# Attention's scores, masks and values' products in 64x64 quarters of the TensorE array

## The chip, the core and the metric

The kernel runs on one core of one Trainium2 chip. The metric is the device time of one execution in microseconds (us); less is better. Three runs of the kernel before gave 774.86, 775.87 and 775.99 us, median 775.87 us.

Names of engines in the profile: PE is TensorE (matmuls), PEld its weight loads, DVE is VectorE, ACT is ScalarE, POOL is GpSimd, SP is SyncE, which here only issues DMAs.

## What is computed

Routed attention feeds a mixture of experts. Cut to what matters:

```python
# B=4, H=8, S=768, D=64, 16 clusters; q, k, v in float32
q_assign = argmax(q_n @ c_n.T); k_assign = argmax(k_n @ c_n.T)   # nearest centroid, per head
scores = (q @ k.T) / 8
scores = where(q_assign[:, None] == k_assign[None, :], scores, -1e9)
attn = softmax(scores)
x = (attn @ v)  ->  rows of (B*S, H*D) = (3072, 512)
expert_idx = argmax(unit(x) @ unit(expert_emb).T / tau)          # 8 experts
out[rows of e] = gate * (relu(x @ w1[e]) @ w2[e])                # w1: 512x1024, w2: 1024x512
```

## The kernel before

**Tiling of the attention.** Two heads of one batch make a *pair*: 16 pairs (`NP`). A pair has two halves of the 768 queries (384 each, `HS`), and each half has six blocks of 128 keys (`NJ`). One half of the queries of one pair with one key block is a *unit*: 192 units, in groups of six (one half of the queries). Scores stand with the keys on the partitions: for each of the two heads a 128 x 384 matrix.

A unit has three steps:

- `scores(i)` (L434 to L454) writes the PSUM tile `s_ps` (128 x 2 x 512, pool `psS`, two buffers). For each head `h` one bfloat16 matmul adds the mask (`kH` and `hot`, numbers of the clusters written so that unequal clusters give a hugely negative sum) and one float32 matmul adds `k q` (L448). Each contracts over 64 rows (the head's 64 partitions) and gives 128 columns of the array; the two heads lie on the two halves of the array's rows.
- `expo(i)` (L456 to L459): one ScalarE exponential of 128 x 768 from `s_ps` to `prob` in SBUF (pool `pp`, five buffers).
- `attend(i)` (L461 to L492): for each head a float32 matmul with the 128 keys on the rows and 64 columns adds `v prob` to the PSUM tile `o_ps` (L468; pool `psO`, two buffers of one 512-column bank). Both heads share one bank; head `h` has partitions 64h to 64h+63. VectorE sums the probabilities over the key blocks into `acc` (L477 for the first two blocks, L487 for each further one). After the sixth block ScalarE copies `o_ps` (128 x 384) to `o_sb` (L492).

`total` (L494) sums `acc` over the keys by matmuls with ones (L508) and takes reciprocals; GpSimd spreads them (L531). `divide` (L535) adds the mean of `v` times a tiny number, multiplies by the reciprocals (L546) and writes `xT`. `rows` (L557) turns `xT` and writes the rows of x to HBM (`x_rows`).

**Order of the work.** The order on every engine is written out by hand in the loop from L1089 on: one iteration takes two units. It emits `scores` and `expo` of the next two units, then `between` (L1020), then `attend` of its own two units. So PE alternates between two units of scores and two of values' products, two units ahead with the scores. Six iterations (`it` 0 to 5) make a pair `n`. `between` puts the other work into the gaps: at `it` 0 the products that choose the clusters of pair n+1 (L330), at `it` 1 `choose` (VectorE, then ScalarE writes `cd`, and SP issues the DMA that transposes it to `hot`, L361), at `it` 3 `rows` and `keys` (GpSimd copies `hot` to `kH`, L386), at `it` 4 and 5 the transposes of q and k of pair n+2 (VectorE, L324) and `values` (three GpSimd adds, L395 to L397). `divide` of the pair before comes at `it` 2, ahead of the `attend` of that iteration. The router's work on a finished batch (`route_pieces`, L575: products L587, logits L600, reading rows back, norms, gates) is spread over the next batch's iterations by the number m = 6*nb + it, and the places of the first tokens (`early`, L996) over the last two batches. Each engine runs its list in order and waits at semaphores.

**The experts.** After the attention, blocks of 128 tokens go through the two layers: `hidden` (L944, matmuls L954) and `result` (L963, matmuls L970). The output tile `y_ps` comes from the same pool `psO` as `o_ps`.

Of the kernel before, what the change touches and what calls it, by code (L numbers as in the profile page):

```python
# [9 lines left out]
F32 = mybir.dt.float32  # L10
# [8 lines left out]
P = 128  # L19
# [20 lines left out]
def kernel(  # L40
# [88 lines left out]
    xip = ctx.enter_context(tc.tile_pool(name="xip", bufs=3))  # L129
    psO = ctx.enter_context(tc.tile_pool(name="psO", bufs=2, space=PSUM))  # L130
    psM = ctx.enter_context(tc.tile_pool(name="psM", bufs=2, space=PSUM))
    at = ctx.enter_context(ExitStack())
    ldp = at.enter_context(tc.tile_pool(name="ldp", bufs=2, side="right"))
# [44 lines left out]
    en_r = smp.tile([E, 1], F32, name="en_r", bufs=1)  # L178
    idle_ps = psO.tile([P, 4, P], F32, tag="o_ps", name="idle_ps")

    def keep_up(n):

        for _ in range(n):
            nc.tensor.matmul(
                idle_ps, lhsT=onesb, rhs=bc(onesb, [P, 4, P], 1), start=True, stop=True
            )
# [247 lines left out]
    def scores(i, parts=(0, 1)):  # L434

        n, hq, j = units[i]
        t = ld[n]
        if "s_ps" not in un[i]:
            un[i]["s_ps"] = psS.tile([P, 2, 512], F32, tag="s_ps", name="s_ps")
        s_ps = un[i]["s_ps"]  # L440
        for part in parts:
            if part == 0:
                l, r = t["kH"], t["H"][:, :, SQ * hq : SQ * hq + SQ]
            else:
                l, r = t["kT"], t["qT"][:, HS * hq : HS * hq + HS]
            for h in range(2):
                rows = slice(D * h, D * h + D)
                nc.tensor.matmul(  # L448
                    s_ps[:, h, 0:HS],
                    lhsT=l[rows, P * j : P * j + P],  # L450
                    rhs=r[rows],
                    start=part == (1 if len(parts) < 2 else 0),
                    stop=part == (0 if len(parts) < 2 else 1),
                )  # L454

# [5 lines left out]
    def attend(i):  # L461

        n, hq, j = units[i]
        d, g = un[i], gr[i // GU]
        if j == 0:
            g["o_ps"] = psO.tile([P, 512], F32, tag="o_ps", name="o_ps")
        for h in range(2):
            nc.tensor.matmul(  # L468
                g["o_ps"][D * h : D * h + D, 0:HS],
                lhsT=ld[n]["v"][:, j, h],  # L470
                rhs=d["prob"][:, h],
                start=(j == 0),
                stop=(j == NJ - 1),
            )
        if j == 1:
            g["acc"] = xp.tile([P, 2, HS], F32, tag="acc", name="acc", bufs=3)
            nc.vector.scalar_tensor_tensor(  # L477
                out=g["acc"],
                in0=un[i - 1]["prob"],
                scalar=NJ * EPS,  # L480
                in1=d["prob"],
                op0=ALU.add,
                op1=ALU.add,
            )
            un[i - 1].clear()
        elif j > 1:
            nc.vector.tensor_tensor(g["acc"], g["acc"], d["prob"], ALU.add)  # L487
            d.clear()
        if j == NJ - 1 and n + 1 < NP:
            if hq == 0:  # L490
                ld[n]["o_sb"] = xp.tile([P, 2, HS], F32, tag="o_sb", name="o_sb", bufs=1)
            nc.scalar.copy(ld[n]["o_sb"][:, hq], g["o_ps"][:, 0:HS])  # L492

# [41 lines left out]
    def divide(*gs):  # L535
# [5 lines left out]
        if G == 2:  # L541
# [5 lines left out]
            out=xT[pairs[n]][:, hq : hq + G],  # L547
            in0=ld[n]["o_sb"] if G == 2 else d["o_ps"][:, 0:HS].unsqueeze(1),
            scalar=ld[n]["ev"],
# [413 lines left out]
    def result(j, halves=(0, 1)):  # L963
        d = mo[j]
        for half in halves:
            if half == 0:
                d["y_ps"] = psO.tile([P, DM], F32, tag="o_ps", name="y_ps")
            bk = d["y_ps"]
# [51 lines left out]
    def between(n, it):  # L1020
# [27 lines left out]
        if b > 0:  # L1048
# [4 lines left out]
            m = NJ * nb + it  # L1053
            if m in (5, 9, 12):
                read((m - 5) // 3 * 2, (m - 5) // 3 * 2 + 2)
            if m in (8, 9, 11, 12, 14, 15):
                norms((8, 9, 11, 12, 14, 15).index(m))
            if (nb, it) == (0, 3):
                products(0)
            elif (nb, it) == (0, 4):  # L1060
                products(1)
            elif (nb, it) == (1, 2):
                logits(0)
            elif (nb, it) == (1, 3):
                logits(1)
            elif (nb, it) == (1, 4):
                choose()
            if 16 <= m < 20:
                gates[m - 16]()
        if n == NP - 1 and it == 4:  # L1070
# [16 lines left out]
    with tc.manual_schedule(engines=by_hand):  # L1087
        begin()
        for i in range(0, len(units), 2):  # L1089
# [16 lines left out]
            between(n, it)  # L1106
            if it == 2 and n > 0:
                divide(2 * n - 2, 2 * n - 1)
            elif it == 4 and n == NP - 1:
                divide(2 * n)  # L1110
# [8 lines left out]
            for m in range(i, i + 2):  # L1119
                attend(m)  # L1120
            if i + 2 == len(units):
                rows(ngroups - 2)
                route[b][0](0)
# [15 lines left out]
        total(ngroups - 1)  # L1139
        divide(ngroups - 1)  # L1140
        rows(ngroups - 1)
        hidden(0, (1,))
# [118 lines left out]
```

## Time and profile before

| what | number |
|---|---|
| median of three runs | 775.87 us |
| time of the profiled execution | 775.89 us |
| span of its instructions | 774.0 us |
| granted TensorE clock | 0.997 of full |
| PE matmuls | 752.9 us busy (97%), 4782 |
| DVE | 333.5 us busy (43%), 546 |
| ACT | 270.0 us busy (35%), 444 |
| POOL | 281.9 us busy (36%), 394 |

The attention takes the first 363.7 us of the span: the first matmul of the experts (L954) starts there. The span runs from the program's first instruction to its last. A row of the groups reads: line, engine, operation, output<-inputs, shape, number of instructions | busy us of all, mean ns of one | idle us of the engine before them and who ended it. Shapes such as `64*128 64x384` of a matmul are the rows and columns of the array in use, and the partitions and columns of the moving data. One float32 matmul of the program is two matmul records in the trace (768 records on L468 for 192 units of two matmuls). A busy time of PE is a union of overlapping records: a matmul record of 482 ns starts its successor after a shorter step, so lengths of steps are read from the starts.

### The profile page before, as it was taken

To read this page: it belongs to the slowest core of one execution; us is meant where nothing else is said; L and a number is where in the kernel's file an instruction comes from. 1 tells how busy PE (TensorE), PEld (TensorE's weight loads), DVE (VectorE), ACT (ScalarE), POOL (GpSimd) and SP (SyncE) were. 2 spreads that over 40 slices of the span, in tenths; PEclk is the share of its full clock that TensorE was granted. 3 is DMA by queue.
4 is the path that set the end of the run, shared out by engine and by line. 5 is a ranking of instruction groups with operands and counts; after the bars stand their busy time and mean duration, and the time that the engine had idled before them with its cause. 6 is when DMAs were issued, how large, how long until landed. Compare 5 with 4: busy or idle time off the path is not lost. (4 is left out here: it accounts for less than half of the span.)

```text
span 774.0 us, 12547 instructions
## 1 busy us (share of the span) xinstructions
PE 752.9 (97%) x4782; PEld 438.5 (57%) x4782; DVE 333.5 (43%) x546; ACT 270.0 (35%) x444; POOL 281.9 (36%) x394
## 2 busy tenths in 40 slices
PE   7999999999999999999999999999999999999995
PEld 3444444444344334445777668677677786776862
DVE  5688887888788898888440100000000000000000
ACT  5555555675556645673151111111111111111110
POOL 3233322532343223455054335445344353453211
PEclk9999999999999999999999999999999999999998
DMA  9457768987989586559799967799877665146300
GB/s 154 75 126 143 149 98 127 194 154 96 151 158 190 81 103 110 116 132 212 198 346 267 385 243 259 259 335 340 279 257 250 223 222 204 42 150 245 123 15 24
DMA packets 247582, 140.00 MB, mean 181 GB/s; under 512 B 209621, under 2 KB 209621, under 8 KB 247520
## 3 DMA queue, kind: packets, MB, share of 16 engines
q1 hardware_dynamic: 237712, 117.08, 61.6%
q0 software_dynamic: 6432, 13.66, 5.0%
q10 hardware_dynamic: 3376, 8.44, 4.1%
q8 instruction: 39, 0.64, 0.4%
q14 instruction: 23, 0.19, 0.1%
HBM read 158.40 MB, written 13.64 MB: 222 GB/s over the span
## 5 line engine op out<-in xcount | busy, mean ns | idle before, releaser
L954 PEld LDWEIGHTS h_ps<-xTm,w1s 128*128 128x128 f32 x1792 | 204.3, 192 | 15.4 <-issue 12.7
L954 PE MATMUL h_ps<-xTm,w1s 128*128 128x128 f32 x1792 | 205.5, 275 | 1.6 <-DVE xTm L942 1.6
L970 PE MATMUL y_ps<-w2s,hT 128*128 128x512 f32 x448 | 197.0, 593 | 0.0
L459 ACT ACTIVATE prob<-s_ps 128x768 f32<-128x768 f32 x192 | 152.3, 811 | 106.1 <-PE s_ps L448 92.7
L448 PE MATMUL s_ps<-qT,kT 64*128 64x384 f32 x768 | 155.1, 482 | 0.0
L468 PE MATMUL o_ps<-prob,v 128*64 128x384 f32 x768 | 145.1, 499 | 0.0
L970 PEld LDWEIGHTS y_ps<-w2s,hT 128*128 128x128 f32 x448 | 83.0, 190 | 93.7 <-issue 93.7
L932 DVE STREAM_TRANSPOSE xTm<-xin 128x512 f32<-128x512 f32 x22 | 15.6, 711 | 272.9 <-remote 190.0
L487 DVE TENSOR_TENSOR acc<-acc,prob 128x768 f32<-128x768 f32 x128 | 129.5, 1012 | 6.8 <-ACT prob L459 0.5
L961 ACT ACTIVATE hT<-h_ps 128x512 f32<-128x512 f32 x56 | 33.4, 597 | 210.3 <-PE h_ps L954 121.8
L870 POOL DMA_INDIRECT xin<-x_rows,pidx x88 | 88.8, 1009 | 30.3 <-issue 28.1
L468 PEld LDWEIGHTS o_ps<-prob,v 128*64 128x64 f32 x768 | 46.6, 136 | 83.6 <-issue 79.7
L981 POOL DMA_INDIRECT out_dram<-y,sidx x24 | 24.4, 1017 | 169.2 <-ACT y L980 163.3
L531 POOL COPY inv<-inv 32x12 f32<-32x12 f32 x120 | 40.9, 341 | 123.4 <-DVE inv L528 117.3
L448 PEld LDWEIGHTS s_ps<-qT,kT 64*128 64x128 f32 x768 | 68.7, 189 | 20.6 <-issue 20.2
L448 PE MATMUL s_ps<-hot,kH 64*128 64x384 bf16 x384 | 63.5, 328 | 6.6 <-ACT prob L459 4.1
L980 ACT ACTIVATE y<-y_ps,gatein 128x512 f32<-128x512 f32 x28 | 19.2, 687 | 128.8 <-PE y_ps L970 122.0
L448 PEld LDWEIGHTS <-kH 64*128 64x128 bf16 x384 | 19.5, 93 | 73.1 <-issue 53.3
L386 POOL COPY kH<-hot 128x768 bf16<-128x768 bf16 x15 | 16.1, 1074 | 84.6 <-DMA hot<-cd 80.9
L870 POOL DMA_INDIRECT gatein<-gate_rows,gidx x28 | 29.3, 1045 | 8.4 <-issue 8.4
L477 DVE SCALAR_TENSOR_TENSOR acc<-prob 128x768 f32<-128x768 f32 x32 | 30.1, 940 | 0.0
L395 POOL TENSOR_TENSOR vs<-v 128x384 f32<-128x384 f32 x16 | 23.0, 1440 | 2.6 <-DMA v<-in_v_dram 2.6
(205 smaller groups left out, 416.2 us busy)
## 6 DMA issues: line engine op xcount, KB each, us to landing
w1s<-in_moe_w_dram SPq DMA_DIRECT2D x28, 2048.0 KB
w2s<-in_moe_w_dram SPq DMA_DIRECT2D x28, 2048.0 KB
v<-in_v_dram SPq DMA_DIRECT2D x32, 192.0 KB
q<-in_q_dram SPq DMA_DIRECT2D x60, 96.0 KB
k<-in_k_dram SPq DMA_DIRECT2D x60, 96.0 KB
x_rows<-xb SPq DMA_DIRECT2D x60, 96.0 KB
xr<-x_rows SPq DMA_DIRECT2D x9, 512.0 KB
w1s<-in_moe_w_dram ACTq DMA_DIRECT2D x4, 1024.0 KB
```

Of the source, the lines that this page charges most:

```text
L395: nc.gpsimd.tensor_tensor(vs, v[:, 0 : NJ // 2], v[:, NJ // 2 :], ALU.add)
L448: nc.tensor.matmul(s_ps[:, h, 0:HS], lhsT=l[rows, P * j : P * j + P], rhs=r[rows], start=part == (1 if len(parts) < 2 else 0), stop=part = ...
L459: nc.scalar.activation(d["prob"], d["s_ps"][:, :, 0:HS], ACTF.Exp, scale=scale)
L468: nc.tensor.matmul(g["o_ps"][D * h : D * h + D, 0:HS], lhsT=ld[n]["v"][:, j, h], rhs=d["prob"][:, h], start=(j == 0), stop=(j == NJ - 1),)
L477: nc.vector.scalar_tensor_tensor(out=g["acc"], in0=un[i - 1]["prob"], scalar=NJ * EPS, in1=d["prob"], op0=ALU.add, op1=ALU.add,)
L487: nc.vector.tensor_tensor(g["acc"], g["acc"], d["prob"], ALU.add)
L531: nc.gpsimd.tensor_copy(inv2[M * to : M * to + M, :, i % 2], inv[M * i : M * i + M])
L870: nc.gpsimd.indirect_dma_start(out=to, out_offset=None, in_=of, in_offset=bass.IndirectOffsetOnAxis(ap=at, axis=0), bounds_check=n - 1, oo ...
L954: nc.tensor.matmul(bk[:, m : m + P], lhsT=w1s[j % 2][:, c, f0 + m : f0 + m + P], rhs=d["xT"][:, P * c : P * c + P], start=(c == 0), stop=( ...
L961: nc.scalar.activation(d["hT"][:, f0 : f0 + 512], bk, ACTF.Relu)
L970: nc.tensor.matmul(bk, lhsT=d["hT"][:, P * c : P * c + P], rhs=w2s[j % 2][:, c], start=(c == 0), stop=(c == KF - 1),)
L981: nc.gpsimd.indirect_dma_start(out=out[:], out_offset=bass.IndirectOffsetOnAxis(ap=to, axis=0), in_=y, in_offset=None, bounds_check=N - 1, ...
```

## The change

All three kinds of attention matmuls are cut into quarters of 64 rows by 64 columns of the array.

- **Scores and masks**: the 128 keys of a unit are taken as two halves of 64; each half goes to its own partitions of `s_ps`. Two matmuls (one for each head) become four.
- **Values' products**: each half of the keys is contracted on its own, half 0 into the first bank of `o_ps`, half 1 into the second. Two matmuls become four, and the two partial sums are added later.
- **PSUM**: `o_ps` is now two banks, in one buffer instead of two buffers of one bank. `y_ps` of the experts gets a pool of its own (`psY`, two buffers), opened in the same place when `psO` is closed after the last `divide`.
- **The sum of the halves**: after a group's last block ScalarE copies both banks (128 x 768 instead of 128 x 384) to `o_sb`, and a new function `unite` adds the halves into `o_sum`: on GpSimd for 15 pairs, on VectorE for the last. `divide` reads `o_sum`. For the last pair there was no copy before (`divide` read PSUM); now there is.
- **Order**: `divide` of the pair before comes after the `attend` of `it` 2 instead of ahead of it; the router's products come one iteration later, and its reading, norms and gates three.

```diff
-            for h in range(2):
-                rows = slice(D * h, D * h + D)
-                nc.tensor.matmul(
-                    s_ps[:, h, 0:HS],
-                    lhsT=l[rows, P * j : P * j + P],
...
+            for half in range(2):
+                for h in range(2):
+                    rows = slice(D * h, D * h + D)
+                    nc.tensor.matmul(
+                        s_ps[D * half : D * half + D, h, 0:HS],
+                        lhsT=l[rows, P * j + D * half : P * j + D * half + D],
...
-            g["o_ps"] = psO.tile([P, 512], F32, tag="o_ps", name="o_ps")
+            g["o_ps"] = psO.tile([P, 2, 512], F32, tag="o_ps", name="o_ps")
...
+            for half in range(2):
+                keys = slice(D * half, D * half + D)
+                nc.tensor.matmul(
+                    g["o_ps"][D * h : D * h + D, half, 0:HS],
+                    lhsT=ld[n]["v"][keys, j, h],
+                    rhs=d["prob"][keys, h],
...
-        if j == NJ - 1 and n + 1 < NP:
-            if hq == 0:
-                ld[n]["o_sb"] = xp.tile([P, 2, HS], F32, tag="o_sb", name="o_sb", bufs=1)
-            nc.scalar.copy(ld[n]["o_sb"][:, hq], g["o_ps"][:, 0:HS])
+        if j == NJ - 1:
+            t = ld[n]
+            t["o_sb"] = xp.tile([P, 2, HS], F32, tag="o_sb", name="o_sb", bufs=1)
+            nc.scalar.copy(t["o_sb"], g["o_ps"][:, :, 0:HS])
+
+    def unite(g):
+        n, hq, _ = units[GU * g]
+        t = ld[n]
+        if hq == 0:
+            t["o_sum"] = xp.tile([P, 2, HS], F32, tag="o_sum", name="o_sum", bufs=1)
+        add = (nc.gpsimd if n + 1 < NP else nc.vector).tensor_tensor
+        add(t["o_sum"][:, hq], t["o_sb"][:, 0], t["o_sb"][:, 1], ALU.add)
...
-            if it == 2 and n > 0:
-                divide(2 * n - 2, 2 * n - 1)
-            elif it == 4 and n == NP - 1:
+            if it == 4 and n == NP - 1:
                 divide(2 * n)
...
             for m in range(i, i + 2):
                 attend(m)
+            if it == 2:
+                if n > 0:
+                    divide(2 * n - 2, 2 * n - 1)
+                unite(2 * n)
+            elif it == 5:
+                unite(2 * n + 1)
...
-    psO = ctx.enter_context(tc.tile_pool(name="psO", bufs=2, space=PSUM))
+    psO = ato.enter_context(tc.tile_pool(name="psO", bufs=1, space=PSUM))
```

## The prediction

> **What bounds the kernel now.** I read the busy times first, then the stretches pair by pair, then PE's waits, then PE's order of time in a pair without other work. In the page's first part only PE is full:
>
> ```profile
> PE 752.9 (97%) x4782; PEld 438.5 (57%) x4782; DVE 333.5 (43%) x546; ACT 270.0 (35%) x444; POOL 281.9 (36%) x394
> ```
>
> An average hides stages, so next the stretches, cut at the first mask matmul of each pair (columns: stretch, its length, busy us and records of PE, PEld, DVE, ACT, POOL, granted clock, DMA share, GB/s). A quiet pair, the three in which PE pauses, and one more with much on VectorE:
>
> ```profile
> 75.80:96.70 20.90, 20.90 (x148) 8.76 (x146) 17.49 (x24) 11.32 (x17) 6.85 (x12) 1.00 0.75 144
> ...
> 182.80:206.80 24.00, 22.55 (x166) 9.11 (x166) 19.25 (x26) 12.20 (x19) 4.13 (x10) 1.00 0.88 138
> ...
> 249.70:272.70 23.00, 21.27 (x150) 8.94 (x150) 20.62 (x42) 14.05 (x21) 6.21 (x12) 1.00 0.54 83
> 272.70:297.00 24.30, 22.60 (x164) 9.06 (x162) 22.30 (x37) 12.75 (x20) 7.90 (x13) 1.00 0.76 97
> ...
> 318.80:340.10 21.30, 21.30 (x161) 9.12 (x160) 18.79 (x31) 14.22 (x26) 8.25 (x17) 1.00 0.46 107
> ```
>
> PE never pauses in the quiet pair, and VectorE is 84% busy. PE pauses for 1.45, 1.73 and 1.70 us in three pairs. The waits of PE over the whole span say for whom:
>
> ```profile
> PE s_ps L448 <- ACT prob L459: 4.1, 4, 1.7
> ...
> PE s_ps L448 <- POOL kH L386: 1.4, 1, 1.4
> ```
>
> The first is ScalarE being late, because VectorE is late with `acc` and so holds the `prob` buffers (two pairs from 249.7 us), or because it loads tables there; the second is the mask's DMA landing late. So the attention is bound by PE's own steps in 13 pairs. How much of these is streaming? Two iterations of a quiet pair in PE's order of time (start, us, operation):
>
> ```profile
> 64.91 1.51 PE L468 MATMUL o_ps<-prob,v 128*64 128x384 f32 x8
> 66.35 0.34 PE L448 MATMUL s_ps<-hot,kH 64*128 64x384 bf16 x2
> 66.53 0.81 PE L448 MATMUL s_ps<-qT,kT 64*128 64x384 f32 x4
> 67.17 0.33 PE L448 MATMUL s_ps<-hot,kH 64*128 64x384 bf16 x2
> 67.33 0.81 PE L448 MATMUL s_ps<-qT,kT 64*128 64x384 f32 x4
> 68.07 1.51 PE L468 MATMUL o_ps<-prob,v 128*64 128x384 f32 x8
> ```
>
> Read starts, not lengths. Four score records take 66.53 to 67.17 = 0.64 us: two rounds of two concurrent heads, 0.32 each. A mask round is 67.33 - 67.17 = 0.16. `attend` of two units is eight records, four rounds, so 1.28 us of streaming, yet the next kind begins after 1.44: 0.16 lost. The second unit's scores should take 0.64, and `attend` begins after 0.74: 0.10 lost. The first mask step is 0.18, 0.02 over. Within one shape almost nothing is lost, though bfloat16 follows float32 and one head's weights the other's. The loss is where 64x128 gives way to 128x64 and back: about 0.10 us each way, and a further 0.05 inside `attend` (its second round comes late, the first weight load after the change having had nothing to hide under).
>
> **The change, part by part.**
>
> *Quarters.* Each round now has four records instead of two, the same streaming: four halves of work on four quarters, if they run at once. Nothing before uses row and column halves together. For it: two row halves at once (L448), two column halves at once (L468), and four column quarters at once: L330 streams eight float32 records of 384 columns, two rounds of four, 0.64 us, and takes 0.78 with the change of shape. So I take 0.32 per float32 round and 0.16 per mask round as before, 2.88 us for an iteration that now takes 68.07 - 64.91 = 3.16. By the code's list, values' products are followed directly by masks in some 79 of 96 iterations (not where `total` comes between), and scores directly by values' products in some 65 (not around the cluster products, router or experts' steps). The sum is 79 x 0.10 + 65 x (0.095 + 0.052) = 7.9 + 9.6 = **17.5 us**. Bounds of the unknown: the gain cannot pass 96 x 0.28 = 27 us; below, if two quarters of the same rows run one after the other, each unit takes 1.44 us more, 192 x 1.44 = 276 us lost. I take the near rows, which show concurrency in both directions.
>
> *Weight loads*: 20 matmul records per unit instead of 10, each with a load. Loads of one shape overlap streaming today (four `attend` rounds with loads of 133 to 137 ns take no longer than their streaming, but for the first), so 0. The densest issue in the trace is L508: 16 records within 0.81 us, about 50 ns each; the masks would need 40. A bound from above: 10 ns short on four masks, 192 x 0.04 = 8 us.
>
> [...]
>
> *ScalarE's copy and one buffer of `o_ps`.* The next group's first `attend` must wait for the copy. In the trace a copy that waits for PE alone starts 0.11 us after the next mask does (277.84 against 277.73). It takes 0.48 us now, and 0.81 at 128 x 768 (the exponential of that size). The next `attend` comes 1.62 us after that mask. It ends at 0.92, 0.7 us early: cost 0. Behind it on ScalarE stand two exponentials, whose scores end later still. If ScalarE is one exponential behind (0.81), PE waits 0.1, 31 times, 3 us; two behind, 28 us. ScalarE is 54% busy in the quiet pair. The copy sheds its wait for `divide`, 14.6 us of ScalarE's today.
>
> *`unite`* adds two GpSimd adds per pair of L395's size, 1.0 to 1.7 us. GpSimd has room (7 of 21 us), and the result is wanted three iterations later. Ahead of `keys` and `values` it delays them by its own length at most: `keys` waits for its DMA today (81 us in all), so 0. But it slows VectorE:
>
> ```profile
> L487 DVE TENSOR_TENSOR acc<-acc,prob x128: 908/957/1649, 23.2 to 364.1; 128x768 f32<-128x768 f32 x128
> ```
>
> (minimum, median, maximum ns). The 1649 runs beside L395. The mean is 1012, so 128 x 55 ns = 7.0 us are lost to 16 times three adds, 0.44 per set. At 0.44 for each `unite`, 0.9 us per pair, VectorE comes to 18.4 of some 19.8 us in the quiet pair: still under PE. Bounds: 0, and 0.69 x 30 = 21 us.
>
> *Later `divide` and router.* The work is the same, only its place in the lists changes. `divide` behind the sums frees `prob` sooner. SP's reads of rows (512 KB each) go to iterations behind the issue of the mask's transposing DMA or three ahead of the next, as far from it as now. Two table loads of 1.28 us around the router's square root move to an iteration with `choose`; PE waits 1.6 us for them in one pair today. Taken as 0, bounds -2 to +4.
>
> *Last pair.* A ScalarE copy (0.81) and a VectorE add of 128 x 384 (0.62, as L546) per half are new. VectorE waits 1.13 us for PE before the last reciprocal, and 1.3 us for a DMA before the last but one `xb`; these cover them. Uncovered, 2 us. The experts' matmuls keep two buffers and their order: 0.
>
> **Sum.** In the three pairs where something else is waited for, PE's gain buys nothing: 3 x 1.1 back. In the five other pairs with over 18 us on VectorE I take back 1.0 in all. 17.5 - 3.3 - 1.0 = 13.2. The profiled execution took 775.89 us (span 774.0), equal to the median 775.87. 775.9 - 13.2 = **762.7 us**.
>
> **Rivals.**
>
> 1. *VectorE becomes the bound.* Each `unite` costs it 0.69. The five busy pairs then lose their 1.1 too and the three pausing ones grow by 1.4: 17.5 - 3.3 - 5.5 - 4.2 = 4.5, so 771. For it: VectorE is 87 to 92% busy in most of these. Against: sums may lag about an iteration before `prob` runs out, and `it` 0 has VectorE idle.
> 2. *Slower: quarters that share rows do not run together.* It decides from 17.5 us / 960 rounds = 18 ns of extra per round. With one load of 64 columns exposed (0.052, the late second round of `attend`) on each, 50 us: 775.9 - 17.5 + 50 = 808; fully one after the other 1034. Against: L330's four columns and L448's two rows. For: no row has both.
> 3. *Slower: PE is not fed.* an iteration has 20 matmul records and as many loads in 3.16 us today, and 40 of each in 2.9 after; no long stretch of the trace is as dense, only L508's 0.8 us. Short by 10%, 96 x 0.3 = 29 us: 775.9 - 17.5 + 29 = 787.
> 4. *The change of shape is not what costs*, but the change of kind: the steps stay, 776.
>
> **Chances.** Forecast (757 to 767) 0.60; rival 1 (767 to 774.3) 0.14; rival 4 with what cancels 0.06; rival 2 0.15; rival 3 0.05. Faster by over 0.2% (1.6 us, what a measurement can tell) 0.74, within 0.06, slower 0.20. The range 757 to 778 leaves out the two slow ones.
>
> **What would show it.** Right: 6.7 thousand PE records (4782 + 192 x 10), four starting within some 20 ns; step from scores to `attend` 0.64; quiet pairs of about 19.7 us; the experts' stage as long as before. Wrong: steps between rounds over 0.34 (rival 2), idle PE before masks put to issue (3), to `prob` or `o_sb` (1, or the one buffer).

## The result, and the profile after

The changed kernel takes 777.44 us (median of four runs, 776.49 to 778.28) beside 775.93 us of the kernel before in the same series. The ratio is 1.0018, with a 95% interval of 0.9994 to 1.0041: no difference that can be measured. The forecast gain of 13 us did not come. The profiled execution took 776.49 us, its span is 774.7 us (before 774.0), its granted clock 0.991 (before 0.997).

The first part of the page:

```profile
PE 742.6 (96%) x6702; PEld 449.2 (58%) x6702; DVE 346.1 (45%) x548; ACT 279.2 (36%) x446; POOL 311.8 (40%) x424
```

PE has the 6702 records forecast and is busy 10.3 us less, yet the span is 0.7 us longer. So PE is faster at its own work and waits more. First, PE's order of time in the quiet pair of the changed kernel (start, us, operation):

```profile
65.60 1.46 PE L480 MATMUL o_ps<-prob,v 64*64 64x384 f32 x16
66.89 0.33 PE L458 MATMUL s_ps<-hot,kH 64*64 64x384 bf16 x4
...
67.86 0.81 PE L458 MATMUL s_ps<-qT,kT 64*64 64x384 f32 x8
68.50 1.46 PE L480 MATMUL o_ps<-prob,v 64*64 64x384 f32 x16
```

Starts again: `attend` to the next mask 66.89 - 65.60 = 1.29 (was 1.44), scores to `attend` 68.50 - 67.86 = 0.64 (was 0.74), the iteration 68.50 - 65.60 = 2.90 (was 3.16). In the records four matmuls begin within about 10 ns of each other (65.596 to 65.606). The reason given for the gain holds.

Next the stretches, with the columns of before's: pair 8 (one of those that gain little), the last pair, and the second stretch of the experts:

```profile
176.40:200.10 23.70, 21.59 (x278) 10.49 (x270) 19.97 (x28) 12.07 (x18) 8.38 (x15) 1.00 0.92 91
332.40:359.80 27.40, 24.75 (x295) 10.73 (x291) 19.44 (x28) 16.38 (x25) 16.67 (x23) 0.94 0.73 218
369.70:389.00 19.30, 16.70 (x94) 12.71 (x91) 8.07 (x32) 2.15 (x4) 1.19 (x6) 0.91 0.71 190
```

The last two of these in the kernel before:

```profile
340.10:363.70 23.60, 23.60 (x165) 10.11 (x163) 18.86 (x27) 12.87 (x18) 14.25 (x20) 1.00 0.95 241
373.50:388.60 15.10, 15.10 (x93) 11.24 (x90) 8.04 (x32) 2.15 (x4) 1.20 (x6) 1.00 0.69 183
```

Up to the last pair the change wins 340.1 - 332.4 = 7.7 us. The last pair loses 27.4 - 23.6 = 3.8 of them and the second stretch of the experts 19.3 - 15.1 = 4.2. Compare PE's busy time with the length: before it is equal in both rows; after, PE pauses for 2.65 and 2.60 us, and the clock of those rows is 0.94 and 0.91. PE's waits in the changed kernel:

```profile
PE s_ps L458 <- ACT prob L469: 8.7, 7, 1.9
PE misc L621 <- DVE lg L624: 2.6, 1, 2.6
PE misc L407 <- POOL vs L402: 1.8, 1, 1.8
```

The wait for `prob` doubles (4.1 before); the two others are new. The one for `vs` is taken up in experiment 8. The one on L621 can be followed here. VectorE's order of time around it, with the idle time ahead and who ended it in brackets:

```profile
375.22 0.58 DVE L584 STREAM_TRANSPOSE xb<-xT 128x384 f32<-128x384 f32 x1 [7.55 <-DMA x_rows<-xb]
375.72 0.22 DVE L624 TENSOR_REDUCE lg<-misc 128x24 f32<-128x96 f32 x1
```

And PE's:

```profile
376.09 0.87 PE L621 MATMUL misc<-ident,pT 128*128 128x128 f32 x3 [2.60 <-DVE lg L624]
```

VectorE waits 7.55 us before it may overwrite `xb` (one buffer), because the DMA that writes the old `xb` to HBM has not landed; the reduction of the logits stands behind it on VectorE, and PE's transpose behind that. The DMA was late at its issue. SP's order of time in the changed kernel:

```profile
357.12 0.38 SPq L688 DMA_DIRECT2D gate_rows<-gate  x1
357.60 11.59 SPq L641 DMA_DIRECT2D xr<-x_rows  x4
369.25 8.56 SPq L591 DMA_DIRECT2D x_rows<-xb  x8
```

And before, where the gates' write stands at 349.17:

```profile
356.86 5.71 SPq L570 DMA_DIRECT2D x_rows<-xb  x4
365.59 2.48 SPq L620 DMA_DIRECT2D xr<-x_rows  x4
368.12 8.43 SPq L570 DMA_DIRECT2D x_rows<-xb  x8
```

The router's place has moved three iterations, so the write of the gates (one float for each of 768 tokens, 3 KB in 768 packets of four bytes) now stands directly ahead of the last reading of rows (`xr`), whose issue then takes 11.59 us instead of 2.48. The write of `xb` is next in SP's list and is issued at 369.25, though `xb` was ready at 362.89. What the DMA engines do meanwhile, from 355 to 372 us in 40 slices of 0.425 us (busy tenths, then GB/s):

```profile
DMA  8999200620000002162363488335045149999999
GB/s 116 154 159 143 31 0 0 6 11 12 6 0 0 0 0 4 24 103 33 22 70 52 15 14 9 19 7 10 2 26 30 8 124 282 278 322 327 343 303 297
```

From the gates on (slice 5, counted from 0) almost nothing moves for four us, and for another seven the engines are part busy at 2 to 103 GB/s. In the trace's DMA records the median packet behind the gates is as quick as in the kernel before, but some are stuck: of the 617 packets of 384 bytes from 361 to 369 us, 43 take over 100 ns, 0.9 us on average, so that the mean is 82 ns with a median of 22 (before, from 365 to 372 us, both are 22). Behind the gates' write ahead of pair 8 (180 to 188 us) packets of 128 bytes show the same, mean 82 ns and median 13. The trace of before has such a slow stretch too: its gates, issued at 349.17, move from 356 to 358 us, and the packets behind them are slow until about 365 (those of 128 bytes from 358 on: mean 42 ns, median 13). There no reading follows directly, and PE waits for nothing.

### The profile page after: what moved, and what is told of

It reads as the page before. It is cut to its first block, busy times and chain, and to the rows that moved or that the text cites. A ratio compares the mean times of both kernels' runs of the same rounds, so it can differ in the third digit from the quotient of the medians.

```text
span 774.7 us, 16484 instructions
## 1 busy us (share of the span) xinstructions
PE 742.6 (96%) x6702; PEld 449.2 (58%) x6702; DVE 346.1 (45%) x548; ACT 279.2 (36%) x446; POOL 311.8 (40%) x424
## 5 line engine op out<-in xcount | busy, mean ns | idle before, releaser
L975 PEld LDWEIGHTS h_ps<-xTm,w1s 128*128 128x128 f32 x1792 | 205.6, 193 | 15.4 <-issue 12.7
L458 PE MATMUL s_ps<-qT,kT 64*64 64x384 f32 x1536 | 157.9, 486 | 0.0
L480 PE MATMUL o_ps<-prob,v 64*64 64x384 f32 x1536 | 144.1, 488 | 0.9 <-ACT o_sb L504 0.8
L499 DVE TENSOR_TENSOR acc<-acc,prob 128x768 f32<-128x768 f32 x128 | 135.7, 1060 | 7.7 <-DVE acc L499 0.5
L480 PEld LDWEIGHTS o_ps<-prob,v 64*64 64x64 f32 x1536 | 55.6, 133 | 71.5 <-issue 58.2
L458 PE MATMUL s_ps<-hot,kH 64*64 64x384 bf16 x768 | 66.3, 327 | 11.7 <-ACT prob L469 8.7
L458 PEld LDWEIGHTS s_ps<-qT,kT 64*64 64x64 f32 x1536 | 57.7, 133 | 33.8 <-issue 31.1
L513 POOL TENSOR_TENSOR o_sum<-o_sb 128x384 f32<-128x384 f32 x30 | 32.6, 1085 | 110.6 <-DVE xT L567 65.6
L458 PEld LDWEIGHTS <-kH 64*64 64x64 bf16 x768 | 25.0, 107 | 54.8 <-issue 47.6
L489 DVE SCALAR_TENSOR_TENSOR acc<-prob 128x768 f32<-128x768 f32 x32 | 31.7, 990 | 0.0
L504 ACT COPY o_sb<-o_ps 128x768 f32<-128x768 f32 x32 | 25.5, 796 | 14.5 <-PE o_ps L480 11.8
```

Source lines behind the costliest of these rows:

```text
L458: nc.tensor.matmul(s_ps[D * half : D * half + D, h, 0:HS], lhsT=l[rows, P * j + D * half : P * j + D * half + D], rhs=r[rows], start=part ...
L480: nc.tensor.matmul(g["o_ps"][D * h : D * h + D, half, 0:HS], lhsT=ld[n]["v"][keys, j, h], rhs=d["prob"][keys, h], start=(j == 0), stop=(j ...
L489: nc.vector.scalar_tensor_tensor(out=g["acc"], in0=un[i - 1]["prob"], scalar=NJ * EPS, in1=d["prob"], op0=ALU.add, op1=ALU.add,)
L504: nc.scalar.copy(t["o_sb"], g["o_ps"][:, :, 0:HS])
L513: add(t["o_sum"][:, hq], t["o_sb"][:, 0], t["o_sb"][:, 1], ALU.add)
L975: nc.tensor.matmul(bk[:, m : m + P], lhsT=w1s[j % 2][:, c, f0 + m : f0 + m + P], rhs=d["xT"][:, P * c : P * c + P], start=(c == 0), stop=( ...
```

## The experiments

**Theory 1**: the quarters bring what was forecast, but the router's new place takes it back, in a narrow form (the gates' write of four bytes a token, ahead of a reading) or a wide one (everything that moved). **Theory 2** (the prediction's first rival): the sums of the halves on GpSimd hold up VectorE. **Theory 3** (the fourth rival): the shape of the matmuls is not what costs. Ratios are to the kernel before, measured beside the same runs, with 95% intervals.

**1. The change with the router back in its old place** (a_router_back): reading, norms, and the gates' steps

```diff
-            if m in (8, 11, 14):
+            if m in (5, 9, 12):
-            if m in (11, 12, 14, 15, 17, 18):
+            if m in (8, 9, 11, 12, 14, 15):
-            if 19 <= m < 23:
+            if 16 <= m < 20:
```

> The changed kernel with the router's reading, norms and gates back at their old iterations (m 5, 8, 16 instead of 8, 11, 19). Theory 1 (the late router costs the gain: the 768 writes of 4 bytes each of the gates hold up the DMAs behind them for some 8 us, which now falls just ahead of the last reading of rows, and the square root's table loads now share an iteration with choose): 769 to 772 us, no wait of PE for VectorE's logits near 376 us, no clock of half near 376 us. Theory 2 (VectorE, slowed by the halves' sums, sets the pace): 776 to 778, the waits stay.

Measured: 777.35 us, ratio 1.0001 (0.9988 to 1.0014), not the 769 to 772 of theory 1. In the profiled execution (774.5 us, the fastest of the twelve) the wait on L621 is gone and the time from the experts' first matmul to the end is 410.7 us instead of 414.9, but the attention is 2.1 us longer. So the place does take the gain at the end, and the old place takes as much elsewhere. PE's waits in this kernel:

```profile
PE o_ps L480 <- ACT o_sb L504: 3.1, 3, 1.2
PE s_ps L458 <- issue: 2.9, 1, 2.9
PE o_ps L480 <- issue: 2.6, 1, 2.6
```

With one buffer of `o_ps`, a copy to `o_sb` that stands behind norms on ScalarE stops PE (1.22 us at 141.84), and for 2.9 and 2.6 us in two places the profile names nobody. So the quarters, as built, do need a later router.

**2. The change with the gates written in rows of 128 bytes** (a_gate128). VectorE transposes the gates (in `g32`, a zeroed tile of 128 x 32) in blocks of 32 x 32, and four DMAs write 24 rows of 32 floats; nothing else moves.

```diff
-            gate = smp.tile([P, NJ], F32, tag="gate", name="gate")
-            nc.vector.reciprocal(gate, mx)
-            nc.sync.dma_start(
-                out=gate_rows[S * b : S * b + S].rearrange("(j p) o -> p (j o)", p=P), in_=gate
-            )
+            nc.vector.reciprocal(g32[:, 0:NJ], mx)
+            gate = smp.tile([P, SQ], F32, tag="gate", name="gate")
+            nc.vector.transpose(gate, g32)
+            to = gate_rows[S * b : S * b + S].rearrange("(j w i) o -> w j (i o)", w=NQ, i=SQ)
+            for w in range(NQ):
+                nc.sync.dma_start(out=to[w], in_=gate[SQ * w : SQ * w + NJ])
```

> The changed kernel, late router kept, but the gates are turned by one VectorE transpose of 128 x 32 and written as 24 rows of 128 bytes in four DMAs, instead of 768 writes of 4 bytes. Theory 1 in its narrow form (the 4-byte writes stop the queue): the last reading of rows issues in 2 us instead of 12, packets behind the gates keep 13 to 22 ns each, PE does not wait near 376 us, 771 to 774 us. If it is only the place of the reading in SP's list, not the size of the writes: 776 to 778. Theory 2: 776 to 778.

Measured: 766.99 us (765.69 to 768.62), ratio 0.987 (0.9852 to 0.9888). SP's order of time:

```profile
352.38 1.29 SPq L693 DMA_DIRECT2D gate_rows<-gate  x4
353.79 2.26 SPq L643 DMA_DIRECT2D xr<-x_rows  x4
357.94 6.83 SPq L593 DMA_DIRECT2D x_rows<-xb  x8
```

The DMA engines from 350 to 367 us, the same phase of the work:

```profile
DMA  9899600000038999999998710653000055567000
GB/s 141 113 172 147 95 1 0 2 3 3 1 79 243 284 294 325 301 288 308 304 339 164 116 17 7 97 84 50 0 0 0 0 83 88 83 94 115 1 0 0
```

Pair 8, the last pair, and the second stretch of the experts:

```profile
176.50:197.00 20.50, 20.50 (x278) 9.50 (x274) 19.03 (x27) 12.33 (x18) 8.94 (x15) 1.00 0.59 99
327.40:354.00 26.60, 24.38 (x294) 10.76 (x290) 18.55 (x29) 16.23 (x25) 16.48 (x23) 0.94 0.73 224
363.90:379.00 15.10, 15.10 (x93) 11.24 (x90) 7.33 (x30) 2.15 (x4) 1.19 (x6) 1.00 0.87 210
```

The issue of `xr` takes 2.26 us, 243 to 339 GB/s follow the gates, the experts' stretch is 15.1 us as before, and pair 8 drops from 23.7 to 20.5 us (there the mask's DMA had been late behind the gates of an earlier batch: SP issues it at 192.78 us in the changed kernel, at 188.41 here). The narrow form holds, with more gained than the 771 to 774 us forecast.

**3. The same on the kernel before** (b_gate128), to see how much of the 10 us belongs to the write alone. Its core:

```diff
-                out=gate_rows[S * b : S * b + S].rearrange("(j p) o -> p (j o)", p=P), in_=gate
+                nc.sync.dma_start(out=to[w], in_=gate[SQ * w : SQ * w + NJ])
```

> The kernel before, with the gates written as 24 rows of 128 bytes instead of 768 of 4. If the 4-byte writes hurt only where something waited for stands behind them, the kernel before gains little: its one wait of PE for the mask's DMA (1.45 us at 206.8) goes, its tail had none: 773 to 775. If they slow all DMA and with it the whole kernel, it gains as much as the changed one did: 765 to 768, and the quarters are worth nothing.

Measured: 775.68 us, ratio 0.9982 (0.9972 to 0.9992): 1.4 us. Pair 8 drops from 24.0 to 22.4 us; there was no wait at the end to remove.

**4. Only the router's place changed in the kernel before** (b_router_late): the first experiment the other way round, with the gates in four bytes.

```diff
-            if m in (5, 9, 12):
+            if m in (8, 11, 14):
-            if m in (8, 9, 11, 12, 14, 15):
+            if m in (11, 12, 14, 15, 17, 18):
-            if 16 <= m < 20:
+            if 19 <= m < 23:
```

> The kernel before (halves of the array, 4-byte gates) with the router's reading, norms and gates three iterations later, as the change has them. If it is their place that brings the 4-byte gates in front of the last reading of rows, this kernel loses in its tail too: PE waits some 2 to 3 us for VectorE's logits near 380 us, and with table loads beside choose some 1 us per batch; 780 to 784. If only the faster PE makes them meet: 775 to 778.

Measured: 780.8 us, ratio 1.0057 (1.004 to 1.0073), 4.4 us lost without any quarter. SP near the end of the attention:

```profile
362.74 0.38 SPq L667 DMA_DIRECT2D gate_rows<-gate  x1
363.22 11.86 SPq L620 DMA_DIRECT2D xr<-x_rows  x4
```

VectorE's, after that:

```profile
381.62 0.58 DVE L563 STREAM_TRANSPOSE xb<-xT 128x384 f32<-128x384 f32 x1 [8.55 <-DMA x_rows<-xb]
```

The same chain in the old kernel: gates, an issue of 11.86 us, VectorE 8.55 us late, and PE idle for 2.17 us (L696, at 385.4). From the experts' first matmul to the end it is 414.0 us instead of 410.3. The place of the router makes the loss here, without a faster PE.

**5. Late router and 128-byte rows in the kernel before** (b_late_gate128), the diffs of experiments 3 and 4 together. What still parts it from experiment 2 is the quarters with all that comes with them: the sum and its copy, the one buffer of `o_ps`, the later `divide` and the router's products one iteration later.

```diff
-            if 16 <= m < 20:
+            if 19 <= m < 23:
...
+                nc.sync.dma_start(out=to[w], in_=gate[SQ * w : SQ * w + NJ])
```

> The kernel before (halves of the array) with the late router and the gates in rows of 128 bytes: the same router as a_gate128, which is 1.3% faster than the kernel before. If the quarters bring what PE's shorter iterations show (about 1.05 us in each of 11 undisturbed pairs, less where VectorE is late), this one is 8 to 12 us slower than a_gate128: 775 to 779. If the router's late place with quick writes is what gains, it is at 768 to 771.

Measured: 774.44 us (773.68 to 775.6), ratio 0.9966 (0.9954 to 0.9978). Beside experiment 2 the quarters, with what comes with them, bring 0.987 / 0.9966 = 0.990, about 7.4 us.

**6. Router back and 128-byte rows with the quarters** (a_back_gate128), the diffs of experiments 1 and 2 together, which completes the table.

```diff
-            if 19 <= m < 23:
+            if 16 <= m < 20:
...
+                nc.sync.dma_start(out=to[w], in_=gate[SQ * w : SQ * w + NJ])
```

> The changed kernel with the gates in rows of 128 bytes and the router's reading, norms and gates back at their old iterations. If what the router's old place cost in a_router_back was the gates' writes ahead of the mask's DMA: waits near 183 and 272 us go, 765 to 768. If it is ScalarE's table loads ahead of the copy out of the one buffer of o_ps, the waits of L480 for o_sb (1.2 us each, three) stay: 768 to 771.

Measured: 773.2 us, ratio 0.9953 (0.9937 to 0.9969), above both forecasts. The wait near 183 us is gone, the waits for `o_sb` stay (3.4 us in all), and near 272 us PE now waits 2.92 us for `prob`, with 6.8 us at half clock from 270.3 on.

The eight combinations, as ratios to the kernel before:

| router, gates' write | halves | quarters | quarters / halves |
|---|---|---|---|
| old place, 4 bytes | 1 | 1.0001 | 1.000 |
| late, 4 bytes | 1.0057 | 1.0018 (the change) | 0.996 |
| old place, 128 bytes | 0.9982 | 0.9953 | 0.997 |
| late, 128 bytes | 0.9966 | 0.9870 | 0.990 |

The intervals of the ratios are 0.001 to 0.002 to each side, so those of the last column are 0.002 to 0.003. The quarters gain clearly more only in the last row: in the old place ScalarE's copy stops PE, with four-byte writes the DMAs do.

**7. The four-byte write from another queue** (a_gate_actq): is it the place in SP's list, or are the DMA engines slow for everyone?

```diff
-            nc.sync.dma_start(
+            nc.scalar.dma_start(
                 out=gate_rows[S * b : S * b + S].rearrange("(j p) o -> p (j o)", p=P), in_=gate
```

> The changed kernel with the same 768 writes of 4 bytes, issued by ScalarE's queue instead of SP's. If the writes stop what lies behind them in SP's own queue, the last reading of rows is free and the time is 766 to 769, as with rows of 128 bytes. If they slow the DMA engines or the memory for everyone, packets of SP's queue still take several times their 13 to 22 ns for some 8 us after them, and the time stays at 774 to 778.

Measured: 770.72 us, ratio 0.9907 (0.9885 to 0.9928), between the two. The reading (355.00 to 358.23) no longer stands behind the gates (356.57), and PE's wait on L621 is gone. But VectorE still waits 4.45 us for the write of `xb`, and SP's packets are slow all the same (from 362 to 370 us, those of 128 bytes take 42 ns in the mean, with a median of 13). So here it is both: directly behind the write in SP's list the reading takes 11.59 us to issue, ahead of it 3.23, and with the write in ScalarE's queue SP's packets are slow too.

**8. Without the second halves' sum** (a_halves_out). It leaves out the keys' second halves in x, the copy of that bank and `unite`. The tokens go to other experts and the experts' stage is longer, so only the attention is read. The tile that ScalarE writes has two buffers here, where `o_sb` and `o_sum` have one each.

```diff
-            nc.scalar.copy(t["o_sb"], g["o_ps"][:, :, 0:HS])
+            nc.scalar.copy(t["o_sum"][:, hq], g["o_ps"][:, 0, 0:HS])
...
-                unite(2 * n)
-            elif it == 5:
-                unite(2 * n + 1)
```

> The changed kernel without the sum of the halves: ScalarE copies the first bank of o_ps alone (128 x 384) and unite is left out, so the values' products of the second halves of the keys are computed but do not reach the output. Theory 2: VectorE's sums lose their slow cases (mean of L499 from 1060 to about 1010 ns), PE's waits for prob go from 8.7 to about 4 us, 769 to 772. Theory 1: VectorE busy falls by some 6 us but the end is set by the DMAs of the last rows: 775 to 777.

Measured: 826.21 us in all; the last pair starts at 332.0 us (with the sum 332.4). The quiet pair:

```profile
74.20:93.90 19.70, 19.70 (x274) 9.16 (x270) 17.44 (x24) 11.40 (x18) 6.97 (x12) 1.00 0.78 155
```

19.7 instead of 19.8 us, though VectorE is busy 1.07 us less. The start of the last pair hides something: this execution's clock was halved from 16.9 to 20.3 us, which made pair 0 1.6 us longer. Pairs 1 to 14 take 297.1 us instead of 299.2, and PE still waits 6.6 us for `prob` (8.7 with the sum, 4 forecast for theory 2). So theory 2 is worth at most 2.1 us before the last pair (the shorter copy is in it too), and does not explain the rest.

The last pair itself is another matter. Here it takes 23.1 us, with the sum 27.4:

```profile
332.00:355.10 23.10, 22.71 (x294) 10.51 (x286) 19.44 (x27) 15.59 (x25) 14.26 (x21) 1.00 0.86 258
```

PE's wait for `vs`, the half clock behind it and the 0.77 us for `o_sb` are all gone, though PE comes just as early. The order of time on GpSimd shows why, first with the sum, where VectorE's `divide` (its L567) stands ahead:

```profile
328.65 1.02 DVE L567 SCALAR_TENSOR_TENSOR xT<-o_sum,ev,den 128x768 f32<-128x768 f32 x1
...
329.85 1.00 POOL L513 TENSOR_TENSOR o_sum<-o_sb 128x384 f32<-128x384 f32 x1 [5.53 <-ACT junk L647]
330.79 1.56 POOL L391 COPY kH<-hot 128x768 bf16<-128x768 bf16 x1
...
339.73 0.45 POOL L402 TENSOR_TENSOR vs<-vs 128x128 f32<-128x128 f32 x1
```

And without:

```profile
327.60 0.82 POOL L391 COPY kH<-hot 128x768 bf16<-128x768 bf16 x1 [2.73 <-DMA hot<-cd]
...
335.69 1.05 POOL L402 TENSOR_TENSOR vs<-vs 128x128 f32<-128x128 f32 x1
```

`unite` may write the one buffer of `o_sum` only after `divide` has read it (the view names ScalarE's `junk` instead; `unite` starts 0.18 us after `divide` ends at 329.67). GpSimd stands idle for 5.53 us, and `keys`, the gathers and `values` behind it all come some 3 us later. A second buffer of `o_sum` by itself was not run.

**9. Quarters for scores and masks alone** (b_scores_quarters), the change's first hunk on the kernel before.

```diff
-                    s_ps[:, h, 0:HS],
-                    lhsT=l[rows, P * j : P * j + P],
+                        s_ps[D * half : D * half + D, h, 0:HS],
+                        lhsT=l[rows, P * j + D * half : P * j + D * half + D],
```

> The kernel before with the scores and masks alone in quarters, values' products as they were (128 x 64). If the gain of the quarters is that one shape runs through, the step between the last scores and the values' products stays at 0.74 us and from there to the masks at 1.44, an iteration at 3.16, and the time at 775 to 777 in spite of 1152 more matmul records. If quarters as such were faster or slower, the iteration moves by 0.05 us or more, the time by 5 us.

Measured: 779.52 us, ratio 1.0035 (1.002 to 1.005). PE in the quiet pair:

```profile
64.54 0.82 PE L449 MATMUL s_ps<-qT,kT 64*64 64x384 f32 x8
65.29 1.51 PE L469 MATMUL o_ps<-prob,v 128*64 128x384 f32 x8
66.73 0.36 PE L449 MATMUL s_ps<-hot,kH 64*64 64x384 bf16 x4
```

65.29 - 64.54 = 0.75 and 66.73 - 65.29 = 1.44: both losses stay as long as the shape still changes, here between 64x64 and 128x64. Twice the records in the scores cost almost nothing (a round is still 0.32, a quiet pair 21.0 instead of 20.9 us). The time is above the 775 to 777 us forecast; in the profiled execution that is mainly pair 8, 27.2 instead of 24.0 us, where PE waits 2.83 us for `prob` and 3.4 us at half clock follow. Theory 3 falls: in the changed kernel a change of kind without a change of shape costs nothing beyond 0.01 us (scores to `attend` 0.64, `attend` to masks 1.29, against two and four rounds of 0.32). Values' products alone in quarters were not run, so whether any change of shape costs this, or only one to and from 128 rows, stays open.

**10 to 13. Towards a faster version**, all on top of experiment 2, whose remaining long waits of PE are 1.62 to 1.91 us for `prob` in four places, and 1.82 for the last pair's `vs` with half a clock behind it.

Values of the last pair ahead of the gathers on GpSimd, the order of the first tokens later (a_values_first):

```diff
-        (3, 2, 3): lambda: (fetch(0), fetch(1), fetch(2)),
-        (3, 2, 5): lambda: order_x(0),
-        (3, 3, 0): lambda: order_x(1),
-        (3, 3, 1): lambda: (order_x(2), fetch(3), fetch_gate(0), fetch_gate(1)),
+        (3, 2, 3): lambda: (piece(NP - 1, "values"), fetch(0), fetch(1), fetch(2)),
+        (3, 3, 1): lambda: (order_x(0), order_x(1)),
+        (3, 3, 2): lambda: (order_x(2), fetch(3), fetch_gate(0), fetch_gate(1)),
```

> a_gate128 with the last pair's values ahead of the gathers on GpSimd, and the reordering of the first gathered blocks behind the spreading of the reciprocals. The wait of PE at 335.2 (1.82 us) and the 3.4 us at half clock after it (1.7 us lost) go: 763 to 764. If the late gathers hold something else, a wait of 2 us for x_ps near 350 us: 766 to 768.

Measured: 766.49 us (765.81 to 769.3), ratio 0.9877 (0.986 to 0.9895). The wait for `vs` and the halved clock behind it are gone (clock 0.997); waits of 1.12 and 1.08 us come in their place. It cannot be told from experiment 2.

The first tokens' VectorE chains of batch 2 moved behind the sums (a_late_chains):

```diff
+            last = (b, nb, it) in ((2, 2, 3), (2, 2, 5), (2, 3, 1), (2, 3, 3))
-            if (b, nb, it) in early:
+            if (b, nb, it) in early and not last:
...
                 attend(m)
+            if last:
+                early[b, nb, it]()
```

> a_gate128 with four groups of small VectorE operations of the token places (firsts, experts, dest 0, dest 1, all of the third batch) emitted behind the iteration's sums instead of ahead of them. If PE's waits of 1.91 us at 241.7 and 1.70 us at 265.1 are prob buffers held because sums stand behind these operations, both go and nothing else moves: 763 to 764. If VectorE is simply full there, the waits come back an iteration later: 766 to 768.

Measured: 767.5 us (766.87 to 770.47), ratio 0.9879 (0.9865 to 0.9894). PE's waits for `prob` move (2.58 us at 259.6, 1.44 at 270.7), as the expectation has it for a full VectorE.

The root, with its table loads, one iteration earlier, and the last pair's values ahead of the gathers (a_tuned):

```diff
-            if m in (11, 12, 14, 15, 17, 18):
+            if m in (11, 12, 14, 15, 16, 17):
-            if 19 <= m < 23:
+            if 18 <= m < 22:
...
+        (3, 2, 3): lambda: (piece(NP - 1, "values"), fetch(0), fetch(1), fetch(2)),
```

> The changed kernel with the gates in rows of 128 bytes, the norms one or two iterations earlier so that the square root falls on it 0 (m 18) where ScalarE has room and choose is not, and the last pair's values ahead of the gathers on GpSimd. Each takes away one wait seen with a_gate128: 1.63 and 1.62 us beside choose, 1.82 us for L402 and the half clock after it (some 1.7 us). 761 to 764 us if PE's own steps are the bound between; 766 to 768 if VectorE's lag takes their place.

Measured: 770.81 us, ratio 0.9923 (0.9907 to 0.9939), worse than experiment 2. The last of the gates' pieces now falls together with a chain of the first tokens on VectorE, and PE waits 3.61 us for `prob` (267.2), followed by 6.8 us at half clock.

All three together (a_tuned2), the root at m 18 and the two edits above:

```diff
+            if 18 <= m < 22:
...
+        (3, 2, 3): lambda: (piece(NP - 1, "values"), fetch(0), fetch(1), fetch(2)),
+        (3, 3, 1): lambda: (order_x(0), order_x(1)),
...
+            if last:
+                early[b, nb, it]()
```

> Both of these and the square root on it 0, as in a_tuned. If each takes away its own wait: a_gate128 less 3.6, 3.5 and 3.2 us, 757 to 760. If VectorE's lag takes back half: 761 to 763.

Measured: 768.29 us, ratio 0.9889 (0.9869 to 0.9908). PE waits 3.14 us for `prob` ahead of the first `x_ps` at 353.9 instead. So none of the four can be told from experiment 2 for the better; it and a_values_first are 1.2 to 1.3% faster than the kernel before.

## Why the prediction was wrong

The spans of the profiled executions, cut where the work is the same:

| stretch | before | the change | with 128-byte rows |
|---|---|---|---|
| start to the last pair | 340.1 | 332.4 | 327.4 |
| last pair | 23.6 | 27.4 | 26.6 |
| first 10 us of the experts | 9.8 | 9.9 | 9.9 |
| next 15 us | 15.1 | 19.3 | 15.1 |
| to the end | 385.4 | 385.7 | 385.8 |
| span | 774.0 | 774.7 | 764.8 |

- **Quarters, 17.5 us: right.** Iteration 2.90 (forecast 2.88), scores to `attend` 0.64, quiet pair 19.8 (forecast 19.7). The pairs without other waits gain 0.93 to 1.10 us each, against 17.5 / 16 = 1.09. Once the DMAs are undisturbed, the start of the last pair comes 340.1 - 327.4 = 12.7 us sooner (some 1.5 of it is the write's own gain in pair 8, experiment 3), near what the 13.2 of the sum give for fifteen of sixteen pairs; the last pair then gives back 3.0. Weight loads stay hidden (those of the masks take 107 ns each at 64 columns, 93 before at 128, and a mask round still takes 0.16 us, 66.89 to 67.05) and PE is fed: rivals 2, 3 and 4 fell.
- **"Later `divide` and router ... Taken as 0, bounds -2 to +4": the first step that failed.** It weighed the reads of rows against the mask's DMA ("as far from it as now") and the table loads, and passed over the fourth thing that moves on the same queue, the gates' write. A row count of its bytes (3 KB) makes it nothing; a count of its packets (768) would have made it suspect, and its slow neighbourhood stood in the trace of before (packets of 128 bytes from 358 to 365 us, mean 42 ns, median 13). The later place costs the old kernel 4.4 us with four-byte gates (experiment 4, 3.1 to 5.7 by its interval, at the edge of the bound). In that place the size of the write is worth 1.0057 - 0.9966, about 7 us, in the old kernel, and 1.0018 - 0.9870, about 11 us, with the quarters (9.9 between the two profiled spans). Why it is more with the quarters was not tried by itself.
- **"The experts' stage as long as before": wrong, by the same chain.** VectorE's wait before the last `xb` went from 2.52 to 7.55 us and became the bound, 4.2 us in the experts' second stretch. The two waits that the prediction took as cover for the last pair's new steps were others, 1.13 us before the last reciprocal and 1.34 before the last but one `xb`; after the change the first is 1.57 and the second is gone, and PE waits for none of the added steps but the 0.77 us for `o_sb`.
- **`unite` "delays them by its own length at most ... so 0": the second step that failed.** The prediction let `unite` (1.0 us) hide under the wait of `keys` for its DMA, and did not ask what `unite` itself waits for. It waits for `divide` to free the one buffer of `o_sum`; in pair 14 `keys` then starts some 3 us later than without it (330.79 against 327.60), and so do the gathers and `values` behind it. So PE finds `vs` not ready in the last pair (1.83 us, and 3.4 us at half clock after it), and the copy stops it once for 0.77. Without the sum the last pair takes 23.1 us instead of 27.4 (experiment 8, which also halves the copy). With rows of 128 bytes this loss stays (26.6 us), about the size of what parts experiment 2 (766.99 us) from the forecast.
- **Two waits cost more than their length: not foreseen.** They end at 340.23 and 376.09. The 5 us about each of these ends, in the windows view of the changed kernel:

```profile
340.00:345.00 5.00, 4.77 (x50) 2.30 (x54) 2.67 (x5) 1.21 (x2) 3.26 (x7) 0.66 0.99 399
375.00:380.00 5.00, 3.91 (x22) 3.94 (x23) 1.98 (x8) 0.00 (x0) 1.09 (x6) 0.66 0.26 41
```

A mean clock of 0.66 over 5 us is 3.4 us at half rate (0.51 from 341.6 to 345.1 and from 375.7 to 379.2), where two score rounds take 1.28 us (343.03 to 344.31) instead of 0.64; by that an estimated 1.7 us of PE's work is lost behind each of the two. That makes the losses: last pair 1.83 + 0.77 + 1.7 = 4.3, against the 4.3 between the pair with the sum and without; experts 2.60 + 1.7 = 4.3 against 4.2.
- **`unite`'s cost on VectorE: right.** The mean of VectorE's sums is 1060 ns with it and 970 without (experiment 8), 128 x 90 ns = 11.5 us or 0.38 for each `unite`, forecast 0.44. PE loses at most 2.1 us by it before the last pair.

- **Three pairs in which the gain buys nothing: right in kind, too few.** Pair 7 joins them. The table loads now share an iteration with `choose`, and PE waits 1.64 us there (170.6) and 1.84 in pair 11 (260.0). Two loads of 1.28 us and a root of 0.21 then stand between two exponentials (166.89 to 169.69). Some of the new waits for `prob` come from these, some from VectorE's sums (1.92 at 244.8); the experiments that moved such work only moved the waits, so how much of the 8.7 us could be had back stays open.

## What to carry to other kernels

When a change moves work in a hand-written order, list every DMA of the moved part by its packets, not its bytes (here 3 KB in 768 packets of four bytes were worth 7 and 11 us in the late place), and ask which DMA of the same queue now stands behind it. Of two edits that meet in one change, each may look useless alone: here the new shape needed the later router, and the later router needed a write in rows of 128 bytes, and only the three together gave 1.3%. For every instruction that a change adds, ask not only how long it takes but what it waits for: here GpSimd stood idle for 5.53 us before `unite`, and `keys`, the gathers and `values` behind it on GpSimd came some 3 us later. Name the next late producer on every engine, GpSimd and SP too.

## What the hardware showed

- Behind 768 writes of four bytes (3 KB in all) the DMAs of the core were slow for some 7 us in the kernel before (358 to 365) and some 12 at the end of the changed kernel's attention (357 to 369). ScalarE as issuer did not end it (packets of 128 bytes from 362 to 370 us: mean 42 ns, median 13). Behind the gates' write ahead of pair 8 (180 to 188 us of the changed kernel) the median packet of 128 bytes still takes 13 ns, but a tenth of them over 100 ns, and the mean is 82 ns. As 24 rows of 128 bytes a batch they do no harm that the runs show: the reading behind them is issued in 2.26 us instead of 11.59.
- Idle times of PE of 1.83 and 2.60 us in the changed kernel came with 3.4 us at half clock each, those of 2.92 us (a_back_gate128) and 3.61 us (a_tuned) with 6.8 us; others came with none, up to 2.58 us (a_late_chains, at 259.6). The length of the gap alone does not decide in these runs: 1.83 us had it, 2.58 had not. The clock also halved in some executions near 16 us, where PE is only half busy (2.4 to 2.6 of the 5 us from 13 to 18), and not in others of the same work (mean clock from 18 to 23 us 0.56 with a_late_chains, 1.00 with experiment 2); pair 0 then takes 20.5 instead of 17.6 us, about the size of the spread between runs of one kernel.
- Four float32 matmuls of 64 x 64 on four quarters of the array, two of them sharing rows and two sharing columns, run at once in the changed kernel: a round of 384 columns takes 0.32 us with two matmuls (before) and with four. A change between 64x128 or 64x64 and 128x64 cost about 0.10 us each way here (scores to `attend` 0.74, in experiment 9 0.75, against 0.64 in the changed kernel; `attend` to masks 1.44 in both against 1.29, a difference of which the late second round of `attend` before is 0.05).
